# Attention before a gated feed-forward: the pairs' probabilities turned by VectorE and eight transfers instead of by TensorE

## The chip, the cores and the metric

The kernel runs on one core of a Trainium2 chip. The metric is the device time of one execution in microseconds, median of three runs; lower is better. TensorE does the matrix products, VectorE (DVE), ScalarE (ACT) and GpSimd (POOL) the rest; SyncE (SP) only issues DMAs.

## What is computed

```python
# q, k, v: (8, 8, 576, 64): batch, heads, tokens, head size; chunks of 64 tokens
scores = q_c @ k_c.T / sqrt(64)            # each chunk attends to itself
attn = exp(scores - max(scores)); attn = attn / (sum(attn) + 1e-9)
out = attn @ v_c
x = out.transpose(0, 2, 1, 3).reshape(4608, 512)
h = x @ w_in                               # 512 x 2048
g = h * clip(h + 3, 0, 6) / 6
return g @ w_out                           # 2048 x 512
```

## The kernel before

The 4608 tokens are nine blocks of 512. The large products run in three passes (L344 to L346) over operands that are split into a high and a low part. Blocks 0 to 2 go first, by ordinary products. The other six go in three pairs, (3, 4), (5, 6) and (7, 8): for a pair, seven products (numbered 1 to 7) on sums of quarters stand for eight, in the first product (with `w_in`) and again in the second (with `w_out`). The weights for that stream in through three `ws` buffers (`fetch`, L451), the operands are `xop` tiles made by `split` (L456 on ACT, L457 on DVE), and the gate is L637 on ACT and L638 on DVE. L605 are the sums of products in PSUM.

An `Attention` object is four heads of a block: 32 scores of 64 by 64. Its steps are `load_qk`, `load_v`, `scores` (32 matmuls, L228), `soft` (maximum L247, difference L249, exponential L251, sum L253, L257, L258, scaling L260, which leaves the probabilities in `e`), a turn of the probabilities, and `values` (32 matmuls, L310). While pair (3, 4) runs through its products, the four attentions of blocks 5 and 6 run between them; during pair (5, 6), those of blocks 7 and 8. These are the eight attentions of the title. For each of them `move` (L272) issues a DMA that copies `e` into the tile `words` (512 KB), so that its type may be fp32r; `turn` (L287) has TensorE transpose that in eight matmuls of 128 by 128 into PSUM (`two`), and `turned` (L293) has ACT copy them back over `e` as `aT`. The other ten attentions, of blocks 0 to 4, have no move and are transposed as float32 (L289). In what follows a pair's attentions are called the first to the fourth.

What runs when is written out by hand: the work of each engine is recorded slot by slot (`at` and `tick`); a slot is six matmuls of 128x512, and whatever is put at a slot is recorded for every engine, its DMAs on SP too, behind the matmuls of that slot. `STEADY` (one row for each of the four attentions) and `MOVES` hold the slots, counted from the pair's start; slots 0 to 55 are the first product, 56 to 111 the second. Each engine runs its own queue strictly in that order. `visit` records the `values` of one attention and behind them the `scores` of the next.

Each DMA counts on one of eight semaphores (`DMAHW0` to `DMAHW7`) in rotation. Before a DMA is issued on one, SP waits until the DMA that held it before, eight issues earlier, has landed.

Of the kernel before, what the change touches and what calls it, by code (L numbers as in the profile page):

```python
# [17 lines left out]
P = 128  # L18
CH = 64
# [50 lines left out]
TEMPS = {"p1": "w0_1", "u2": "w1_1", "u4": "w2_1"}  # L70
STEADY = ((-0.9, 8.1, 6.1, 0.2, 12.4, 13.9, 17.0, 19.1, 20.1), (13.1, 20.3, 20.1, 22.0, 23.5, 28.5, 32.2, 40.1, 41.1), (29.3, 53.1, 41.1, 42.4, 44.5, 46.4, 49.9, 54.1, 71.8), (65.6, 79.6, 71.8, 75.8, 77.2, 79.4, 79.5, 86.1, 87.6))
NEXT = (-37.5, -17.0, -24.4, -21.4, -18.0, -14.0, 0.5)
MOVES = (10.4, 33.1, 51.2, 79.8)
UNITS = (-2.9, -1.9, -1.8, -1.7, 4.0, 3.9, 5.4, 10.5, 12.5, 12.0, 13.2, 13.5, 16.6, 14.9, 15.4, 17.3, 25.9, 26.1, 27.5, 28.2, 28.5, 32.8, 35.3, 37.1, 39.2, 41.1, 39.3, 43.0)
# [6 lines left out]
def tile_kernel(ctx: ExitStack, tc: tile.TileContext, qk_in, v_in, weights, out):  # L81
# [105 lines left out]
    class Attention:  # L187


        def __init__(self, n, dp, psum=None):  # L190
# [5 lines left out]
            self.moved = None  # L196

# [19 lines left out]
        def scores(self, k=None):  # L217

            t = self.psum("a" if k == "a" else "s").rearrange("p a (c t) -> p a c t", t=CH)
            chunks = range(NB) if k is None else range(NB)[CHUNKS[k]]  # L220
            if k is None:
                self.s = t
            else:
                self.part[k] = t[:, :, :len(chunks)]
            for i, c in enumerate(chunks):
                for a, rows in enumerate(HALF):
                    for o in HALF:
                        PE.matmul(t[o, a, i, :], lhsT=self.qk[rows, c // 2, 0, c % 2, o],  # L228
                                  rhs=self.qk[rows, c // 2, 1, c % 2, o], start=not self.by_product or i == 0,
                                  stop=not self.by_product, skip_group_check=self.by_product)  # L230
# [31 lines left out]
        def subtract(self, k):  # L262

            for a in range(2):
                t = self.part[k][:, a]
                PE.matmul(t, lhsT=ident, rhs=self.m[:, a, CHUNKS[k]].unsqueeze(2).broadcast_to(list(t.shape)),
                          start=False, stop=True, skip_group_check=True)

        def move(self):

            self.moved = slot_tile("w3_1", [P, 2, NT], F32R, "words")
            nc.sync.dma_start(out=self.moved.bitcast(F32), in_=self.e.rearrange("p a c t -> p a (c t)"))  # L272

# [5 lines left out]
        def turn(self, heads):  # L279
            if heads[0] == 0:  # L280
                self.tp = self.psum("t").rearrange("p a (i t) -> p a i t", t=P)
                self.aT = self.e.rearrange("p a c t -> p (a c t)").rearrange("p (a i t) -> p a i t", a=2, t=P)
            for a in heads:
                for i in range(NB // 2):
                    o = slice(i * P, i * P + P)
                    if self.moved is not None:
                        PE.transpose(out=self.tp[:, a, i].bitcast(F32R), in_=self.moved[:, a, o], identity=unit_r[0])  # L287
                    else:
                        PE.transpose(out=self.tp[:, a, i], in_=self.e[:, a].rearrange("p c t -> p (c t)")[:, o], identity=ident)  # L289

# [9 lines left out]
        def multiply(self, heads):  # L300
# [5 lines left out]
            for a in heads:  # L306
                for i in range(NB // 2):
                    for s, rows in enumerate(HALF):
                        for o in HALF:
                            PE.matmul(self.po[s][o, a, i, :], lhsT=self.v[rows, a, i, o], rhs=self.aT[rows, a, i, o], start=True, stop=True)  # L310

# [71 lines left out]
    order.enter_context(tc.manual_schedule())  # L383
    unit_r = []

# [115 lines left out]

    lead = [Attention(n, 0) for n in range(NSTD + 2, NBLK, 2)]
    chain = [Attention(*which) for which in ((2, 0), (2, 1), (3, 0), (3, 1), (4, 0), (4, 1))] + lead[:1]
# [103 lines left out]
    def put_steady(first, base):  # L607

        pair = (first - NSTD) // 2 - 1
        four = [lead[pair]] + [Attention(first + k // 2, k % 2, steady_psum) for k in range(1, 2 * NDP)] + lead[pair + 1:pair + 2]  # L610
        rows = STEADY + (tuple(2 * SLOTS + t for t in NEXT),)
        for k, a in enumerate(four):
            soft = lambda i, a=a: lambda: a.soft(i)
            load_qk, load_v, scores, high, sub, total, mult, turn, values = (base + t for t in rows[k] + (0,) * (9 - len(rows[k])))
            if k:
# [7 lines left out]
                at(mult, soft(4))  # L623
            if len(rows[k]) < 9:
                return
            at(base + MOVES[k], a.move)
            at(turn, a.transpose)
            if k + 1 < len(four) and rows[k + 1][2] == rows[k][-1]:
# [25 lines left out]
    def first_products(box):  # L654
# [7 lines left out]
        for k, (n, ft) in enumerate(MIDDLE):  # L662
# [17 lines left out]
            if late:  # L680
                mm2(*late.pop(0))
                if not late:
                    std.close()
                    pools["L"] = ctx.enter_context(tc.tile_pool(name="late_l", bufs=1, reuse_waits="tile"))
                    unit_r.append(slot_tile("L", [P, P], F32R, "unit"))
                    ACT.copy(out=unit_r[0], in_=ident)
            tick(slot + 1)
# [239 lines left out]
```

## Time and profile before

| | |
|---|---|
| median of 3 runs | 785.77 us (784.89 to 786.03) |
| span of the profiled execution | 782.5 us |
| PE busy | 774.9 us, 99% of the span |
| DVE, ACT, POOL busy | 615.0 (79%), 375.6 (48%), 148.6 us (19%) |
| largest groups on PE | the three passes of the pairs' products, 608 matmuls of 128x512 in each line with `acc`, about 390 ns of latency each |

No time is given for the profiled execution as a whole other than its span, from the first instruction to the last; the median of the runs is 3.3 us above that. In a profile a matmul's duration is a latency, since matmuls are pipelined: what a matmul costs is the distance from its start to the next one's start.

### The profile page before, as it was taken

To read this page: it belongs to the slowest core of one execution; us is meant where nothing else is said; L and a number is where in the kernel's file an instruction comes from. 1 tells how busy PE (TensorE), PEld (TensorE's weight loads), DVE (VectorE), ACT (ScalarE), POOL (GpSimd) and SP (SyncE) were. 2 spreads that over 40 slices of the span, in tenths; PEclk is the share of its full clock that TensorE was granted. 3 is DMA by queue.
4 is the path that set the end of the run, shared out by engine and by line. 5 is a ranking of instruction groups with operands and counts; after the bars stand their busy time and mean duration, and the time that the engine had idled before them with its cause. 6 is when DMAs were issued, how large, how long until landed. Compare 5 with 4: busy or idle time off the path is not lost.

```text
span 782.5 us, 13689 instructions
## 1 busy us (share of the span) xinstructions
PE 774.9 (99%) x5601; PEld 636.9 (81%) x5601; DVE 615.0 (79%) x748; ACT 375.6 (48%) x494; POOL 148.6 (19%) x134
## 2 busy tenths in 40 slices
PE   8999999999999999999999999999999999999998
PEld 5888787888888888888888888888888888888886
DVE  7997868989699968686898886777997756669961
ACT  6997645535456434443654523444644323346330
POOL 0000013365471222322300002221100012221000
PEclk9999999999999999999999999999999999999999
DMA  9997977656867889976776778676756765665573
GB/s 367 408 408 258 345 258 262 238 177 218 334 251 276 295 291 330 347 270 213 268 268 226 258 230 272 220 262 209 263 195 216 247 217 188 194 202 209 183 240 115
DMA packets 50430, 200.12 MB, mean 256 GB/s; under 512 B 4544, under 2 KB 9152, under 8 KB 37312
## 3 DMA queue, kind: packets, MB, share of 16 engines
q1 hardware_dynamic: 50080, 198.99, 72.4%
q8 instruction: 44, 0.72, 0.4%
q10 hardware_dynamic: 288, 0.26, 0.1%
q14 instruction: 18, 0.15, 0.1%
HBM read 152.04 MB, written 42.99 MB: 249 GB/s over the span
## 4 chain that ended last, share of the span: by engine, by line
PE 95%; DVE 2%; DMA 2%; ACT 1%; issue 0%; SPq 0%; ACTq 0%
PE acc L344 23%; PE acc L346 22%; PE acc L345 22%; PE h L344 7%; PE h L346 7%; PE h L345 7%; PE h L310 2%; PE two L228 2%; PE two L289 1%; DMA x<-qk_in 1%; DMA a<-w 1%; PE two L287 1%; DVE w L182 0%; DVE e L260 0%; DVE u L168 0%; PE two L310 0%
## 5 line engine op out<-in xcount | busy, mean ns | idle before, releaser
L344 PE MATMUL acc<-xop,ws 128*128 128x512 f32 x608 | 237.9, 391 | 0.0
L346 PE MATMUL acc<-xop,ws 128*128 128x512 f32 x608 | 236.6, 389 | 0.0
L345 PE MATMUL acc<-xop,ws 128*128 128x512 f32 x608 | 236.6, 389 | 0.0
L344 PEld LDWEIGHTS acc<-xop,ws 128*128 128x128 f32 x608 | 114.1, 188 | 23.9 <-DVE g L638 0.3
L346 PEld LDWEIGHTS acc<-xop,ws 128*128 128x128 f32 x608 | 114.1, 188 | 23.6
L345 PEld LDWEIGHTS acc<-xop,ws 128*128 128x128 f32 x608 | 114.1, 188 | 23.4
L457 DVE TENSOR_TENSOR xop<-g,xop 128x1024 fp32r<-128x1024 f32 x96 | 117.1, 1252 | 18.9 <-ACT xop L456 18.9
L456 ACT CAST xop<-g 128x1024 fp32r<-128x1024 f32 x96 | 97.3, 1053 | 41.7 <-PE acc L346 25.8
L429 POOL TENSOR_TENSOR hl<-hl 128x256 f32<-128x256 f32 x64 | 56.8, 890 | 221.4 <-DVE hl L416 138.7
L723 POOL TENSOR_TENSOR g<-g 128x512 f32<-128x512 f32 x24 | 32.8, 1368 | 327.9 <-DVE g L638 327.9
L637 ACT ACTIVATE r<-acc,half 128x512 f32<-128x512 f32 x100 | 66.4, 687 | 57.8 <-DVE acc L605 42.2
L638 DVE SCALAR_TENSOR_TENSOR g<-r,acc 128x512 f32<-128x512 f32 x100 | 66.2, 680 | 29.7 <-ACT r L637 29.7
L344 PE MATMUL h<-xop,ws 128*128 128x512 f32 x176 | 68.7, 390 | 0.0
L346 PE MATMUL h<-xop,ws 128*128 128x512 f32 x176 | 68.5, 389 | 0.0
L345 PE MATMUL h<-xop,ws 128*128 128x512 f32 x176 | 68.5, 389 | 0.0
L637 ACT ACTIVATE r<-h,half 128x512 f32<-128x512 f32 x28 | 19.3, 690 | 99.6 <-DVE h L605 97.7
L605 DVE TENSOR_TENSOR u<-h,p 128x512 f32<-128x512 f32 x32 | 22.1, 690 | 36.6 <-PE h L346 27.1
L344 PE MATMUL acc<-x,w 128*128 128x512 f32 x112 | 44.7, 399 | 0.0
L346 PE MATMUL acc<-x,w 128*128 128x512 f32 x112 | 43.7, 390 | 0.0
L345 PE MATMUL acc<-x,w 128*128 128x512 f32 x112 | 43.7, 390 | 0.0
L251 ACT ACTIVATE e<-e 128x1024 f32<-128x1024 f32 (+1 forms) x18 | 18.3, 1014 | 43.8 <-DVE e L249 43.7
L346 PEld LDWEIGHTS h<-xop,ws 128*128 128x128 f32 x176 | 33.0, 188 | 6.9
(112 smaller groups left out, 1196.9 us busy)
## 6 DMA issues: line engine op xcount, KB each, us to landing
ws<-b SPq DMA_DIRECT2D x56, 1024.0 KB, 5.1
ws<-a SPq DMA_DIRECT2D x24, 1024.0 KB, 5.5
ws<-a SPq DMA_DIRECT2D x24, 768.0 KB, 5.0
qk<-qk_in SPq DMA_DIRECT2D x16, 1024.0 KB, 8.3
w<-w_in_out SPq DMA_DIRECT2D x12, 1024.0 KB, 17.3
v<-v_in SPq DMA_DIRECT2D x17, 512.0 KB, 6.2
out_t<-o SPq DMA_DIRECT2D x30, 256.0 KB, 6.2
b<-hl SPq DMA_DIRECT2D x12, 512.0 KB, 4.4
```

The costliest lines, as they stand in the source:

```text
L228: PE.matmul(t[o, a, i, :], lhsT=self.qk[rows, c // 2, 0, c % 2, o], rhs=self.qk[rows, c // 2, 1, c % 2, o], start=not self.by_product or i ...
L251: ACT.activation(out=flat(self.e), in_=src if self.by_product else flat(self.e), func=AF.Exp, scale=SCALE)
L344: PE.matmul(ps, lhsT=a_h, rhs=b_h, start=first, stop=False, skip_group_check=more)
L345: PE.matmul(ps, lhsT=a_h, rhs=b_l, start=False, stop=False, skip_group_check=more)
L346: PE.matmul(ps, lhsT=a_l, rhs=b_h, start=False, stop=last, skip_group_check=more)
L429: POOL.tensor_tensor(out=to, in0=x, in1=y, op=op)
L456: ACT.copy(out=t[:, :, 0], in_=src)
L457: DVE.tensor_tensor(out=t[:, :, 1], in0=src, in1=t[:, :, 0].bitcast(F32), op=ALU.subtract)
L605: return lambda: DVE.tensor_tensor(out=out, in0=x, in1=y, op=ALU.add)
L637: return (lambda: ACT.activation(out=r, in_=ps, func=AF.Relu, bias=half, scale=1.0 / 6.0), lambda: DVE.scalar_tensor_tensor(out=out, in0=r ...
L638: lambda: DVE.scalar_tensor_tensor(out=out, in0=r, scalar=1.0, in1=ps, op0=ALU.min, op1=ALU.mult))
L723: sub = lambda o, x, y: lambda: POOL.tensor_tensor(out=o, in0=x, in1=y, op=ALU.subtract)
```

## The change

For the eight attentions, the DMA into `words`, the eight transposes on TensorE and the copy on ACT go, and with them the fp32r unit matrix and the copy that made it. In their place `swap` has VectorE turn every 32 by 32 block of `e` in one instruction into a tile `t` (in the same slot of memory that `words` had), and `move` issues eight DMAs on SP, each of 32 partitions by 512 elements (64 KB), that put the turned blocks back over `e`, on the partitions where they belong. `scores` places the 64 by 64 blocks differently for that (as many matmuls, of the same sizes), and `values` reads each operand of 64 columns in two runs of 32. `SWAPS` and `MOVES` give the slots of the two steps; the loading of `q` and `k` of the fourth attention moves from slot 65.6 to 60.5.

```diff
-STEADY = (..., (65.6, 79.6, 71.8, 75.8, 77.2, 79.4, 79.5, 86.1, 87.6))
+STEADY = (..., (60.5, 79.6, 71.8, 75.8, 77.2, 79.4, 79.5, 87.6))
-MOVES = (10.4, 33.1, 51.2, 79.8)
+SWAPS = (7.5, 33.0, 61.9, 79.9)
+MOVES = (10.4, 35.1, 63.2, 80.8)
...
+            if self.blocks:
+                for g in range(NB):
+                    o, i = HALF[g // (NB // 2)], g % (NB // 2)
+                    for a, rows in enumerate(HALF):
+                        for c, to in enumerate(HALF):
+                            PE.matmul(t[to, a, g, :], lhsT=self.qk[rows, i, 0, c, o], rhs=self.qk[rows, i, 1, c, o], start=True, stop=True)
+                return
...
+        def swap(self, tag="w3_1"):
+            t = slot_tile(tag, [P, 2, 2 * NB, CH // 2], F32, "t")
+            DVE.transpose(out=t.rearrange("p j g t -> p g j t"), in_=self.e.rearrange("p a c (j t) -> p (a c) j t", j=2))
+            self.swapped = t.rearrange("p j g t -> p j (g t)")
+
         def move(self):
-            self.moved = slot_tile("w3_1", [P, 2, NT], F32R, "words")
-            nc.sync.dma_start(out=self.moved.bitcast(F32), in_=self.e.rearrange("p a c t -> p a (c t)"))
+            to = self.e.rearrange("p a c t -> p (a c t)").rearrange("p (i t) -> p i t", i=2)
+            for i in range(2):
+                for s in range(2):
+                    for j in range(2):
+                        rows = [slice(s * CH + k * CH // 2, s * CH + (k + 1) * CH // 2) for k in (i, j)]
+                        nc.sync.dma_start(out=to[rows[1], i], in_=self.swapped[rows[0], j])
+            self.aT = to.rearrange("p i (a o c t) -> p a c o i t", a=2, o=2, c=NB // 2)
...
-                            PE.matmul(..., rhs=self.aT[rows, a, i, o], start=True, stop=True)
+                            PE.matmul(..., rhs=self.aT[rows, a, i, HALF.index(o)] if self.blocks else self.aT[rows, a, i, o], start=True, stop=True)
...
+            at(base + SWAPS[k], a.swap)
             at(base + MOVES[k], a.move)
-            at(turn, a.transpose)
```

Line numbers of the changed kernel are some 13 to 15 higher behind the new lines: L344 to L346 are L360 to L362 there, L310 is L326, L457 is L472, L768 is L781, L451 is L466.

TensorE's queue where the first attention of blocks 5 and 6 is turned and used (`two<-unit,words` are the transposes, `h<-e,v` the values, `two<-qk` the scores of the next), before and now:

```order
L345 MATMUL acc<-xop,ws 128x512
L346 MATMUL acc<-xop,ws 128x512
L287 MATMUL two<-unit,words 128x128 x8
L344 MATMUL acc<-xop,ws 128x512
L345 MATMUL acc<-xop,ws 128x512
L346 MATMUL acc<-xop,ws 128x512
L344 MATMUL acc<-xop,ws 128x512
L345 MATMUL acc<-xop,ws 128x512
L346 MATMUL acc<-xop,ws 128x512
L310 MATMUL h<-e,v 64x64 x32
L228 MATMUL two<-qk 64x64 x32
```

```order
L361 MATMUL acc<-xop,ws 128x512
L362 MATMUL acc<-xop,ws 128x512
L360 MATMUL acc<-xop,ws 128x512
L361 MATMUL acc<-xop,ws 128x512
L362 MATMUL acc<-xop,ws 128x512
L326 MATMUL h<-e,v 64x64 x32
L231 MATMUL two<-qk 64x64 x32
```

The eight transposes are gone; nothing else on TensorE has another place.

VectorE's queue in the second product, around the new turn for the third attention (`g<-t` are differences between operands of the products, L768 then and L781 now), before and now:

```order
L768 TENSOR_TENSOR g<-t_3209,g 128x1024
L457 TENSOR_TENSOR xop<-g,xop 128x2x512
L768 TENSOR_TENSOR g<-t_3210,g 128x1024
L457 TENSOR_TENSOR xop<-g,xop 128x2x512
L768 TENSOR_TENSOR g<-t_3211,g 128x1024
```

```order
L781 TENSOR_TENSOR g<-t_3207,g 128x1024
L472 TENSOR_TENSOR xop<-g,xop 128x2x512
L781 TENSOR_TENSOR g<-t_3208,g 128x1024
L280 STREAM_TRANSPOSE t<-e 128x16x2x32
L472 TENSOR_TENSOR xop<-g,xop 128x2x512
L781 TENSOR_TENSOR g<-t_3209,g 128x1024
```

The turn (L280) stands behind the third of four such differences, and everything behind it is one instruction later.

SP's queue at the same place, with the semaphores that each DMA waits for (PE: a buffer that TensorE must have left), before and now:

```order
L451 DMA ws<-b 128x2048 [waits DMAHW6_49,PE_49]
L451 DMA ws<-b 128x2048 [waits DMAHW7_49,PE_49]
L451 DMA ws<-b 128x2048 [waits DMAHW1_49,PE_49]
L203 DMA qk<-qk_in 128x2048
L451 DMA ws<-b 128x2048 [waits DMAHW3_49,PE_49]
```

```order
L204 DMA qk<-qk_in 128x2048
L466 DMA ws<-b 128x2048 [waits DMAHW6_49,PE_49]
L290 DMA e<-t 32x512 [waits DVE_49]
L290 DMA e<-t 32x512 x2
L290 DMA e<-t 32x512 [waits DMAHW7_49]
L290 DMA e<-t 32x512 [waits DMAHW0_49]
L290 DMA e<-t 32x512 [waits DMAHW1_49]
L290 DMA e<-t 32x512 [waits DMAHW2_49]
L290 DMA e<-t 32x512 [waits DMAHW3_49]
L466 DMA ws<-b 128x2048 [waits DMAHW4_49,PE_49]
```

The eight transfers stand between two loads of weights here, the first waits for VectorE's turn, the others at most for the earlier holder of their semaphore, and `qk` has moved ahead of a load. (The one DMA of the third attention before, `words<-e`, stood in the first product.)

## Rows read from the trace of the kernel before

**Rows 1.** The page's first two parts; below, busy time in two stretches.

```profile
PE 774.9 (99%) x5601; PEld 636.9 (81%) x5601; DVE 615.0 (79%) x748; ACT 375.6 (48%) x494; POOL 148.6 (19%) x134
...
298.00:476.00 178.00, 178.00 (x1278) 147.71 (x1277) 142.21 (x171) 78.72 (x103) 29.94 (x26) 1.00 0.76 263
313.00:332.50 19.50, 19.50 (x211) 16.21 (x210) 12.96 (x20) 8.18 (x13) 7.08 (x8) 1.00 0.95 347
```

**Rows 2.** Timeline of PE, a first attention: start us, us, engine, line, operation, tiles.

```profile
325.66 0.39 PE L346 MATMUL acc<-xop,ws 128*128 128x512 f32 x1
325.89 0.80 PE L287 MATMUL two<-unit,words 128*128 128x128 f32 x8
326.52 0.46 PE L344 MATMUL acc<-xop,ws 128*128 128x512 f32 x1
326.82 0.40 PE L345 MATMUL acc<-xop,ws 128*128 128x512 f32 x1
...
328.05 1.16 PE L310 MATMUL h<-e,v 64*64 64x64 f32 x64
329.04 1.11 PE L228 MATMUL two<-qk 64*64 64x64 f32 x64
```

**Rows 3.** Instructions of L287: ns min/median/max, first and last start in us.

```profile
L287 PE MATMUL two<-unit,words x64: 221/249/253, 325.9 to 590.7; 128*128 128x128 f32 x64
```

**Rows 4.** Timeline of DVE where the third attention's turn will stand.

```profile
395.56 1.21 DVE L768 TENSOR_TENSOR g<-t,g 128x1024 f32<-128x1024 f32 x1
396.70 1.21 DVE L457 TENSOR_TENSOR xop<-g,xop 128x1024 fp32r<-128x1024 f32 x1
```

**Rows 5.** Timeline of PE: values of the third and the fourth attention.

```profile
403.36 1.16 PE L310 MATMUL h<-e,v 64*64 64x64 f32 x64
...
428.09 1.16 PE L310 MATMUL h<-e,v 64*64 64x64 f32 x64
```

**Rows 6.** Timeline of SP's queue: the kernel's first nine issues, later ones at the worst.

```profile
0.74 0.86 SPq L209 DMA_DIRECT2D qk<-qk_in  x2
...
3.69 1.52 SPq L149 DMA_DIRECT2D w<-w_in_out  x3
...
92.88 1.07 SPq L401 DMA_DIRECT2D b<-w  x1
```

**Rows 7.** DMA issues: count, size of one, median us from issue to landing.

```profile
out_t<-o SPq DMA_DIRECT2D x2, 128.0 KB, 1.7
...
ws<-b SPq DMA_DIRECT2D x56, 1024.0 KB, 5.1
```

**Rows 8.** Timeline of DVE: the fourth attention's scaling.

```profile
417.94 1.22 DVE L260 TENSOR_TENSOR e<-e,z 128x1024 f32<-128x1024 f32 x1
```

**Rows 9.** Timeline of SP's queue, a first attention, each with its landing in us.

```profile
313.84 0.32 SPq L451 DMA_DIRECT2D ws<-a  x1
...
DMA to landing us min/median/max: 7.2/7.2/7.2
318.29 0.55 SPq L203 DMA_DIRECT2D qk<-qk_in  x1
...
DMA to landing us min/median/max: 9.1/9.1/9.1
```

**Rows 10.** Timeline of SP's queue, a second attention; landing in us; PE's values there.

```profile
349.45 0.33 SPq L451 DMA_DIRECT2D ws<-a  x1
...
DMA to landing us min/median/max: 8.1/8.1/8.1
...
359.59 1.16 PE L310 MATMUL h<-e,v 64*64 64x64 f32 x64
```

**Rows 11.** Timelines of DVE and PE where the first attention's turn will stand.

```profile
311.64 0.69 DVE L638 SCALAR_TENSOR_TENSOR g<-r,acc 128x512 f32<-128x512 f32 x1 [0.17 <-ACT r L637]
...
313.28 0.69 DVE L605 TENSOR_TENSOR u<-acc,u 128x512 f32<-128x512 f32 x1
...
315.00 0.39 PE L344 MATMUL acc<-xop,ws 128*128 128x512 f32 x1
```

More of the change, by code (lines that the diff above doesn't have):

```diff
@@ L70 @@
 TEMPS = {"p1": "w0_1", "u2": "w1_1", "u4": "w2_1"}
-STEADY = ((-0.9, 8.1, 6.1, 0.2, 12.4, 13.9, 17.0, 19.1, 20.1), (13.1, 20.3, 20.1, 22.0, 23.5, 28.5, 32.2, 40.1, 41.1), (29.3, 53.1, 41.1, 42.4, 44.5, 46.4, 49.9, 54.1, 71.8), (65.6, 79.6, 71.8, 75.8, 77.2, 79.4, 79.5, 86.1, 87.6))
+STEADY = ((-0.9, 8.1, 6.1, 0.2, 12.4, 13.9, 17.0, 20.1), (13.1, 20.3, 20.1, 22.0, 23.5, 28.5, 32.2, 41.1), (29.3, 53.1, 41.1, 42.4, 44.5, 46.4, 49.9, 71.8), (60.5, 79.6, 71.8, 75.8, 77.2, 79.4, 79.5, 87.6))
 NEXT = (-37.5, -17.0, -24.4, -21.4, -18.0, -14.0, 0.5)
-MOVES = (10.4, 33.1, 51.2, 79.8)
+SWAPS = (7.5, 33.0, 61.9, 79.9)
+MOVES = (10.4, 35.1, 63.2, 80.8)
 UNITS = (-2.9, -1.9, -1.8, -1.7, 4.0, 3.9, 5.4, 10.5, 12.5, 12.0, 13.2, 13.5, 16.6, 14.9, 15.4, 17.3, 25.9, 26.1, 27.5, 28.2, 28.5, 32.8, 35.3, 37.1, 39.2, 41.1, 39.3, 43.0)
@@ L187, in tile_kernel, with __init__ @@
     class Attention:
-        def __init__(self, n, dp, psum=None):
+        def __init__(self, n, dp, psum=None, blocks=False):
+            self.blocks = blocks
             self.n, self.dp = n, dp
@@ L195, in __init__ @@
             self.by_product = False
-            self.moved = None
         def load_qk(self, qk=None):
@@ L285, in turn @@
                     o = slice(i * P, i * P + P)
[L286 to L289, printed above, removed]
+                    PE.transpose(out=self.tp[:, a, i], in_=self.e[:, a].rearrange("p c t -> p (c t)")[:, o], identity=ident)
         def turned(self, heads):
@@ L309, in multiply @@
                         for o in HALF:
-                            PE.matmul(self.po[s][o, a, i, :], lhsT=self.v[rows, a, i, o], rhs=self.aT[rows, a, i, o], start=True, stop=True)
+                            PE.matmul(self.po[s][o, a, i, :], lhsT=self.v[rows, a, i, o], rhs=self.aT[rows, a, i, HALF.index(o)] if self.blocks else self.aT[rows, a, i, o], start=True, stop=True)
         def multiplied(self, heads):
@@ L383, in tile_kernel @@
     order.enter_context(tc.manual_schedule())
-    unit_r = []
     words = dram.tile([P, NFP, 2, 512], F32, name="words")
@@ L500, in visit @@
         a.multiplied(range(2))
-    lead = [Attention(n, 0) for n in range(NSTD + 2, NBLK, 2)]
+    lead = [Attention(n, 0, blocks=True) for n in range(NSTD + 2, NBLK, 2)]
     chain = [Attention(*which) for which in ((2, 0), (2, 1), (3, 0), (3, 1), (4, 0), (4, 1))] + lead[:1]
@@ L609, in put_steady @@
         pair = (first - NSTD) // 2 - 1
-        four = [lead[pair]] + [Attention(first + k // 2, k % 2, steady_psum) for k in range(1, 2 * NDP)] + lead[pair + 1:pair + 2]
+        four = [lead[pair]] + [Attention(first + k // 2, k % 2, steady_psum, True) for k in range(1, 2 * NDP)] + lead[pair + 1:pair + 2]
         rows = STEADY + (tuple(2 * SLOTS + t for t in NEXT),)
@@ L613, in put_steady @@
             soft = lambda i, a=a: lambda: a.soft(i)
-            load_qk, load_v, scores, high, sub, total, mult, turn, values = (base + t for t in rows[k] + (0,) * (9 - len(rows[k])))
+            load_qk, load_v, scores, high, sub, total, mult, values = (base + t for t in rows[k] + (0,) * (8 - len(rows[k])))
             if k:
@@ L623, in put_steady @@
                 at(mult, soft(4))
-            if len(rows[k]) < 9:
+            if len(rows[k]) < 8:
                 return
+            at(base + SWAPS[k], a.swap)
             at(base + MOVES[k], a.move)
-            at(turn, a.transpose)
             if k + 1 < len(four) and rows[k + 1][2] == rows[k][-1]:
@@ L684, in first_products @@
                     pools["L"] = ctx.enter_context(tc.tile_pool(name="late_l", bufs=1, reuse_waits="tile"))
-                    unit_r.append(slot_tile("L", [P, P], F32R, "unit"))
-                    ACT.copy(out=unit_r[0], in_=ident)
             tick(slot + 1)
```

## The prediction

> **What bounds the kernel now.** I read the page's first part first: PE is busy 774.9 of the 782.5 us span, DVE 615.0 [rows 1]. In the stretch of the first four of the eight attentions, 298 to 476 us, PE is busy all 178.00 of 178.00 us at a granted clock of 1.00 (the upper of its two levels, 2.4 GHz), with DVE at 147.71 and the DMA engines at 0.76 [rows 1]. But busy PE is no proof that nothing waits, so I read the starts. Where nothing but 128x512 products runs, each starts 0.227 us after the one before (the row of L345 to the row of L346 would be 327.05 behind 326.82), and I found no larger step from 298 to 640 us except beside the attentions. So PE, and PE's queue alone, sets the end of this stretch: what leaves PE comes back in full, what DVE, ACT and SP gain is worth nothing, and what they lose costs only from where PE has to wait for it. The whole question is therefore whether the values (L310), the one place where PE meets the new path, find the turned probabilities in time.
>
> **Removed: 64 transposes.** L346 starts at 325.66, the eight transposes follow, and L345 starts at 326.82 with L344 ahead of it [rows 2]. That is 1.16 us for three steps, of which the two of products are 2 x 0.227. The eight transposes cost 1.16 - 0.45 = 0.71 us of PE. There are 64 instructions of L287 [rows 3], eight in each of the eight attentions: 8 x 0.71 = **5.65 us off the path**. The copy on ACT (L293) and the one 512 KB DMA into `words` go too; nobody waits for either, so I give nothing for them. `scores` and `values` keep their matmuls, as many of the same size. Values now read their moving operand as two runs of 32 elements. No row shows that form. A gain I exclude, since the count of columns is the same; half the rate would add what the 32 matmuls of the values take now, 329.04 - 328.05 = 0.99 us less the gap ahead of the scores, some 0.9 us each time [rows 2]. The transposes themselves and the products read longer runs and stream at a column a cycle, and 64 elements already are short runs; I take 0, and 0.9 as the bound.
>
> **Added on DVE: one turn.** No row of before shows a transpose on DVE. The nearest rows are others of 128x1024 in float32: 1.22 us for the scaling L260, 1.21 for L457, which start 1.14 apart [rows 4, 8]. Below it cannot well be, as it writes as many elements; the bound above is a turn at half the pace, 2.4 us. I take 1.2. At the first attention it stands ahead of the sums L605, about 311.5 us: DVE's queue there has small gaps, and the sum that starts at 313.28 would come about 0.6 us later; PE needs it at 315.00 [rows 11], which leaves about 1.0 us over its end of 313.97. Covered by 0.4 us, and not covered at 2.4 us, where some 0.8 us would show once. At the others DVE works 1.9 us or more ahead of PE. ACT and POOL see only a DVE that is 1.2 us later.
>
> **Added on SP: eight issues instead of one.** Each takes time on SP's queue, and PE waits for four of them ahead of the first values matmul and for the other four ahead of the third. The price of one: the only runs of issues in a row without waits are the first nine of the kernel, from 0.74 to 3.69 + 1.52 = 5.21 us [rows 6]: 4.47 / 9 = 0.50 us. A later one took 1.07 us at the worst [rows 6]. I take 0.50, keep 1.07 as the upper bound and, from the first two of the nine (0.86 us for both), 0.43 as the lower. From issue to landing: the smallest transfers are `out_t` of 128 KB, 1.7 us; a `ws` of 1 MB takes 5.1 [rows 7]. For 64 KB I take 1.7, since they are nearer to the first.
>
> **The third attention is where it gets late.** The turn stands ahead of the L457 at 396.70 [rows 4] and ends at 396.70 + 1.22 = 397.92. The first swap is issued then, the eighth 7 x 0.50 = 3.48 later at about 401.4 and landed at 403.1. The values stood at 403.36 [rows 5], and the first two attentions' transposes are no longer ahead of them, nor this one's: counted from the stream's own beginning of this attention, PE arrives 0.71 earlier, at 402.65 (what went before shifts DVE and SP alike). So PE waits 403.13 - 402.65 = 0.48 us. The same place comes in the second pair. **2 x 0.48 = 0.96 us given back.** The loads of `ws` behind the eight swaps are held about 3.8 us; two tiles' use (a tile serves 24 matmuls: 2 x 24 x 0.227 = 10.9 us) less a landing of 5.1 [rows 7] less 3.8 leaves 2.0 us. Covered.
>
> **The fourth.** The scaling of 417.94 [rows 8] is pushed by the third's turn (1.14), since DVE has no gap between; it and the new turn end at about 421.45. Eight issues and a landing: 421.45 + 3.48 + 1.7 = 426.65. PE's values stood at 428.09 [rows 5]; less two sets of transposes and plus the third's wait, that is 428.09 - 1.42 + 0.48 = 427.15. In time by 0.5 us.
>
> **The first and the second.** Here the eighth swap waits on the semaphore of a `ws` load issued just ahead. At the first attention that load went out at 313.84 and landed 7.2 us later, at 321.04 [rows 9]; before, SP issued the next `ws` and `qk` at about 318, so these come about 3 us later. That `qk` (318.29, 9.1 us to land, so 327.40) is wanted by the scores at 329.04 - 0.71 = 328.33 [rows 2, 9], 0.93 us to spare. Taken at its word that is 2.1 us of waiting, but the 9.1 us are a backlog: the engines are busy 0.95 of 313 to 332.5 us at 347 GB/s [rows 1], so a transfer put in later waits less in the backlog. I take 0; the bound is 2.8 us, once, since the second pair has over 1 us to spare. At the second attention the load of 349.45 lands at 357.55 and the values stood at 359.59 [rows 10]: the eighth swap lands by 357.55 + 1.7 = 359.25 against 359.59 - 0.71 = 358.88. At most 0.4 us; without `words` in the same backlog, 0. I take 0.
>
> **Sum.** -5.65 + 0.96 = -4.7 us: a span of 782.5 - 4.7 = 777.8. The median of the runs, 785.77, stands 3.3 us above the span of the profiled execution, and I carry that: **781.1 us**.
>
> Beside this, what the Trainium skill holds against such a change. The rows show transfers that overlap: the loads of 313.84 and the ones behind it are in flight together [rows 9]. The Trainium skill, "DMA: Bandwidth & Descriptors", § Rules for kernel authors, says that transfers under 64 KB mostly pay overhead and should be joined, and that two transfers to disjoint partition halves serialize, so that one of 128 partitions should be used. The swaps, of 64 KB and a quarter of the partitions each, stand at the edge of both; what one behind the other would make of the time is the fourth rival.
>
> **Rivals.** (1) *The gain is eaten up at DVE.* If a turn takes 2.4 us, the third comes out 0.48 + 1.2 late, the fourth about 0.7 less than another turn's 1.2 plus the first delay, some 1.3, the first of the first pair 0.8: 2 x 1.68 + 2 x 1.3 + 0.8 = 6.8 at the worst, and 5.5 where the waits at the third move PE away from the fourth; 785.77 - 5.65 + 5.5 = 785.6. For: no row shows the form. Against: every 128x1024 form in the rows takes 1.2 [rows 4, 8]. The first attention's `qk` (2.8) would end near there too, at 783.9. (2) *Slower: SP's issues are dear.* At 1.07 us each, the eight of the third attention end 7 x (1.07 - 0.50) = 4.0 us later, so PE waits 4.5 there and, the fourth being pushed no further, that is 2 x 4.2 more: 781.1 + 8.4 less what the fourth keeps free, 788.5. It decides from a wait of 2.83 per pair, or 0.48 + 7 x 0.34: from 0.83 us an issue on. For: a late issue took 1.07, and the landing is a guess by which 0.5 more counts double. Against: the issues of one queue without waits averaged 0.50 [rows 6]. (3) *Slower: values at half rate*: 8 x 0.9 = 7.2, 788.3. (4) *Slower: the eight land one behind the other*: 8 x 1.7 = 13.6 instead of 5.2 us from the turn, 8.4 more at the third and, less its 0.5 to spare, some 4 more at each other place: 2 x (8.4 + 3 x 3.5) less what overlaps, about +27, so near 808. Against: the load of 313.84 and the `qk` 4.45 us behind it were both in flight until 321.04 [rows 9].
>
> **How the numbers follow.** The forecast has 0.60, with its own range of 779.5 (issues at 0.43, which takes the third's wait to 0.48 - 7 x 0.07 = 0: 785.77 - 5.65 = 780.1, and half a microsecond of the runs' spread) to 783.5 (0.5 us more at the thirds, the second's 0.4, the `qk`). Rival 1 has 0.22: 783.5 to 787. Rival 2 has 0.12, rivals 3 and 4 0.03 each. About 0.2% (1.57 us, 784.2 to 787.3) is what a measurement of this kernel can tell from no change. Faster: 0.60 and 0.09 of rival 1, 0.69; same: 0.13 of rival 1; slower: 0.18 of the rest. The range takes in the forecast and rival 1, 779.5 to 787.0: 0.82.
>
> **What would show it right or wrong.** The L346 ahead of a first attention's old transposes should be followed by the next product 0.227 us later. The turn should be 1.2 us and not 2.4. The eight issues at the third attention should stand about 0.50 apart, the eighth landing 1.7 later, and the first values matmul there some 0.5 us late, with a releaser among the DMAs; values of the first, second and fourth should start on the stream's step. The values should still take about 0.9 us. Wrong it would be made by a wait of PE at the scores behind the first values (`qk`), by a `ws` that lands late behind the swaps, or by issues that wait on a semaphore that I have taken as free.

## The result, and the profile after

The changed kernel takes 790.39 us in the median (788.75 to 793.39, 8 runs) against 785.9 us before (784.62 to 788.82, 8 runs): a ratio of 1.0055, 95% interval 1.0034 to 1.0077. It is 4.5 us slower, where 4.7 us of gain were forecast, and lies outside the range.

The page's first part and the stretch with the first four of the eight attentions, to be read beside [rows 1] (start and end us, length, then busy us of PE, PEld, DVE, ACT, POOL, PE's granted clock, DMA share, GB/s):

```profile
PE 775.6 (98%) x5537; PEld 635.2 (80%) x5537; DVE 624.2 (79%) x756; ACT 367.7 (47%) x485; POOL 148.6 (19%) x134
...
298.00:476.00 178.00, 172.15 (x1219) 141.45 (x1218) 143.43 (x169) 73.98 (x96) 28.33 (x24) 0.99 0.75 255
```

PE was busy for all of that stretch before; now it stands still for 5.85 of 178 us, and a little of the rest runs at a lower clock. What it waits for, from the view of waits (engine, line, what ended the wait: us in total, times, longest):

```profile
PE h L326 <- DMA e<-t: 2.9, 4, 0.9
PE h L360 <- issue: 1.8, 1, 1.8
PE two L231 <- DMA qk<-qk_in: 1.6, 1, 1.6
PE h L326 <- DVE g L653: 0.7, 1, 0.7
PE h L326 <- issue: 0.3, 1, 0.3
```

The same view of the kernel before has no row there at all. I take each place apart in order. The size of a loss is the distance of starts from the last product ahead of the values to the first one behind the scores, less the 2.34 us that it was before. All losses are those of one profiled execution.

**The first attention.** SP's queue with the landing of `qk`, then PE's:

```profile
315.85 0.32 SPq L466 DMA_DIRECT2D ws<-a  x1
316.26 7.49 SPq L290 DMA_DIRECT2D e<-t  x8
...
324.42 0.46 SPq L204 DMA_DIRECT2D qk<-qk_in  x1
...
DMA to landing us min/median/max: 7.6/7.6/7.6
...
329.35 1.16 PE L326 MATMUL h<-e,v 64*64 64x64 f32 x64
332.15 1.16 PE L231 MATMUL two<-qk 64*64 64x64 f32 x64 [1.65 <-DMA qk<-qk_in]
```

The eight issues hold SP for 7.49 us, since the last of them waits until the load of 315.85 has landed. `qk`, which went out 4.45 us behind that load in [rows 9], now goes out 8.57 us behind it. It lands 7.6 us after its issue instead of 9.1 [rows 9], so 1.5 of the 4.1 us come back, and the scores wait for the rest. The values themselves start on time. Loss: 1.87 us.

**The second attention:**

```profile
352.61 0.32 SPq L466 DMA_DIRECT2D ws<-a  x1
352.98 9.17 SPq L290 DMA_DIRECT2D e<-t  x8
...
DMA to landing us min/median/max: 2.0/7.3/8.8
...
362.76 0.33 PE L326 MATMUL h<-e,v 64*64 64x64 f32 x4 [0.45 <-DMA e<-t]
363.80 1.09 PE L326 MATMUL h<-e,v 64*64 64x64 f32 x58 [0.71 <-DVE g L653]
```

The landing times are those of the eight `e<-t`. Each lands behind the loads that are already in the queues, 7.3 us after its issue in the median, and the eighth is not issued before the load of 352.61 is in, at 361.6. The second wait is put down to DVE's gate, but it is the eighth transfer that comes then (361.6 + 2.0 = 363.6). Loss: 1.55 us.

**The third attention.** DVE, SP with the landing of the eight, PE:

```profile
400.88 1.23 DVE L280 STREAM_TRANSPOSE t<-e 128x1024 f32<-128x1024 f32 x1
...
402.14 4.94 SPq L290 DMA_DIRECT2D e<-t  x8
407.19 1.03 SPq L466 DMA_DIRECT2D ws<-b  x2
...
DMA to landing us min/median/max: 1.9/2.0/2.0
...
407.37 0.33 PE L326 MATMUL h<-e,v 64*64 64x64 f32 x4 [0.34 <-issue]
408.59 1.09 PE L326 MATMUL h<-e,v 64*64 64x64 f32 x58 [0.89 <-DMA e<-t]
```

The turn takes 1.23 us, as a neighbour did in [rows 4]. SP waits for it, then issues the eight in 4.94 us; the engines are nearly empty, and each lands 2.0 us after its issue. The eighth is there at 408.5, PE came for it at 406.95. Loss: 1.63 us here and 1.94 us at the same place of the second pair. Behind the eight, two loads of weights go out at once.

**A stop that no semaphore explains.** Nine products behind the scores, in a row of products that wait for nothing (PE, then two stretches of 1 us in the columns above, then a row of the DMA queues from 412 to 414 us: packets, MB, share):

```profile
412.55 0.39 PE L362 MATMUL h<-xop,ws 128*128 128x512 f32 x1
414.75 0.50 PE L360 MATMUL h<-xop,ws 128*128 128x512 f32 x1 [1.81 <-issue]
...
416.64 0.63 PE L360 MATMUL h<-xop,ws 128*128 128x512 f32 x1
...
413.00:414.00 1.00, 0.00 (x0) 0.00 (x0) 1.00 (x2) 0.00 (x0) 0.00 (x0) 1.00 1.09 434
...
416.00:417.00 1.00, 1.00 (x3) 0.78 (x3) 1.00 (x2) 0.00 (x0) 0.00 (x0) 0.50 0.50 197
...
q8 instruction: 1, 0.02, 2.8%
```

The next product starts 2.20 us behind the last instead of 0.23. While PE stands, the DMA engines are full (1.09, 434 GB/s), and in that time one packet of 16 KB on a queue of instructions (q8) goes through. Soon after PE resumes, its granted clock falls to 0.50, the lower of its two levels (1.2 GHz), and eight products run at 0.427 us a step instead of 0.227. Loss: 1.97 us for the stop and 1.70 behind it, of which the eight products are 1.60.

The sum: 1.87 + 1.55 + 1.63 + 1.94 + 1.97 + 1.70 = 10.7 us lost, 5.65 won: 5.0 slower, beside 4.5 by the medians. All other visits (the fourth of each pair, the first and second of the second pair) run as before, in 2.34 us, or 1.41 at the very last, which has no scores behind it. The spans differ by more, 789.9 and 782.5: the profiled execution of the changed kernel was 2.0 us behind at the first of the eight attentions already, where the two kernels do the same, and 0.4 are left over.

### The profile page after: what moved, and what is told of

The parts are those of the page before. It is cut to its first block, busy times and chain, and to the rows that moved or that the text cites. A ratio compares the mean times of both kernels' runs of the same rounds, so it can differ in the third digit from the quotient of the medians.

```text
span 789.9 us, 13685 instructions
## 1 busy us (share of the span) xinstructions
PE 775.6 (98%) x5537; PEld 635.2 (80%) x5537; DVE 624.2 (79%) x756; ACT 367.7 (47%) x485; POOL 148.6 (19%) x134
## 4 chain that ended last, share of the span: by engine, by line
PE 87%; DVE 4%; DMA 4%; SPq 1%; issue 1%; ACT 1%; DVEq 0%; ACTq 0%
PE acc L360 21%; PE acc L362 20%; PE acc L361 20%; PE h L360 7%; PE h L362 7%; PE h L361 7%; DMA w<-w_in_out 3%; PE h L326 2%; SPq L290 1%; DVE xop L472 1%; PE two L231 1%; DMA qk<-qk_in 1%; PE two L305 1%; PE two L236 1%; DVE g L653 1%
## 5 line engine op out<-in xcount | busy, mean ns | idle before, releaser
L360 PE MATMUL acc<-xop,ws 128*128 128x512 f32 x608 | 237.6, 391 | 0.0
L362 PE MATMUL acc<-xop,ws 128*128 128x512 f32 x608 | 236.6, 389 | 0.0
L360 PEld LDWEIGHTS acc<-xop,ws 128*128 128x128 f32 x608 | 114.1, 188 | 24.9 <-DVE g L653 0.8
L362 PEld LDWEIGHTS acc<-xop,ws 128*128 128x128 f32 x608 | 114.2, 188 | 23.5
L472 DVE TENSOR_TENSOR xop<-g,xop 128x1024 fp32r<-128x1024 f32 x96 | 116.9, 1248 | 17.0 <-ACT xop L471 17.0
L360 PE MATMUL h<-xop,ws 128*128 128x512 f32 x176 | 69.4, 394 | 1.8 <-issue 1.8
L361 PE MATMUL h<-xop,ws 128*128 128x512 f32 x176 | 69.2, 393 | 0.0
L362 PE MATMUL h<-xop,ws 128*128 128x512 f32 x176 | 69.2, 393 | 0.0
L360 PE MATMUL acc<-x,w 128*128 128x512 f32 x112 | 44.7, 399 | 0.0
L362 PE MATMUL acc<-x,w 128*128 128x512 f32 x112 | 43.7, 390 | 0.0
L360 PEld LDWEIGHTS h<-xop,ws 128*128 128x128 f32 x176 | 33.5, 190 | 9.3 <-issue 2.2
```

The costliest lines, as they stand in the source:

```text
L360: PE.matmul(ps, lhsT=a_h, rhs=b_h, start=first, stop=False, skip_group_check=more)
L361: PE.matmul(ps, lhsT=a_h, rhs=b_l, start=False, stop=False, skip_group_check=more)
L362: PE.matmul(ps, lhsT=a_l, rhs=b_h, start=False, stop=last, skip_group_check=more)
L472: DVE.tensor_tensor(out=t[:, :, 1], in0=src, in1=t[:, :, 0].bitcast(F32), op=ALU.subtract)
```

## Experiments

The theory after these rows: all that was lost goes back to the eight issues on SP, to the wait for the load ahead of them, and to the loads behind them. The rivals were VectorE's turn, the new form of values and scores, and the DMA engines themselves.

**No transfers.**

```diff
...
-                        nc.sync.dma_start(out=to[rows[1], i], in_=self.swapped[rows[0], j])
-            self.aT = to.rearrange(...)
+            self.aT = self.swapped.rearrange(...)
```

> The eight transfers of each attention are left out; VectorE's turn stays, and the values read the turned tile itself, so part of the output is wrong (the blocks are not swapped). Theory (SP's queue): everything lost comes from the eight issues on SP, the waits for them and the loads that they hold, so without them the 5.65 us of the transposes come back in full: about 780.2 us, ratio 0.993, no wait of PE at the values. Rival 1 (VectorE): the turn delays the operands of the products; then the time stays above 784 us and PE waits for DVE. Rival 2 (the reading in two runs of 32, or the new order of the scores, is slower): the values or the scores take more than 2.34 us together and the time stays above 784 us.

Measured: 779.39 us, ratio 0.9933 (0.9916 to 0.9950). The view of PE's waits is empty again. The first stretch:

```profile
298.00:476.00 178.00, 178.00 (x1258) 146.97 (x1257) 149.44 (x179) 74.68 (x99) 30.91 (x26) 1.00 0.74 252
```

DVE does more in it than before (149.44 against 142.21 us) and PE waits for nothing. The visits take the old 2.34 us. The turn is free, and the form of values and scores is too. Both rivals fall, and the first term of the prediction stands: the transposes are worth their 5.65 us, within the interval.

**Transfers that nobody waits for.** All eight are issued, the values read the turned tile:

```diff
-            self.aT = to.rearrange(...)
+            self.aT = self.swapped.rearrange(...)
```

> All eight transfers are issued as in the changed kernel, but the values read VectorE's turned tile and not what the transfers bring, so PE waits for none of them (part of the output is wrong for that). Theory (SP's queue): two kinds of loss, the values' own waits (about 1.5 us at the second attention, 1.6 and 1.9 at the two third ones, 5.1 in all) and loads that the burst holds on SP (1.9 us at the scores behind the first attention, and the stop of 2 us behind the third with 1.6 us at half clock). Only the first kind goes: 790.4 - 5.1 = about 785.3 us (784 to 786.5). Rival (the wait is all): 780.2 us, as without transfers.

Measured: 781.31 us, ratio 0.9959 (0.9943 to 0.9974), 4 us better than expected and within 1.1 us of the rival's 780.2. PE's waits are these:

```profile
PE two L231 <- DMA qk<-qk_in: 1.1, 1, 1.1
PE h L360 <- DVE o L800: 0.3, 1, 0.3
```

The late `qk` remains, 1.34 us by the starts: the burst alone costs that. The other losses go with the values' waits, as the rival said. The stop behind the third attention, which I had counted with the held loads, is not there, though the loads go out in a bunch here too. So it needs more than the burst.

**The instruction stream cut elsewhere.** The warming products at the kernel's start, in four pieces each:

```diff
-            PE.matmul(idle, lhsT=a[:, :P], rhs=b, ...)
+            for k in range(4):
+                PE.matmul(idle[:, k * P:k * P + P], lhsT=a[:, :P], rhs=(columns k * P to k * P + P of b), ...)
```

> The changed kernel with each of the warming products of 512 columns at the kernel's start cut into four of 128 columns: the same columns on PE, but about a hundred more instructions ahead of everything else, so that the stream of instructions is cut at other places where it is loaded. Theory (the stop of 2 us behind the third attention, in a row of products that wait for no semaphore, is a load of instructions that came late while the DMA engines were full): the stop goes or moves to another place, and with it the 1.6 us at half clock; 787 us. Rival (the stop belongs to the loads of weights held by the burst): it stays behind the third attention, 790.4 us.

Measured: 788.51 us, ratio 1.0036 (1.0020 to 1.0051). In the profiled execution the stop of the first pair is gone. In the second pair one has come at the like place, where the changed kernel has none, and this time the clock stays at 1.00:

```profile
573.07 0.39 PE L362 MATMUL h<-xop,ws 128*128 128x512 f32 x1
574.74 0.50 PE L363 MATMUL h<-xop,ws 128*128 128x512 f32 x1 [1.28 <-issue]
```

The order of all work is the same; ahead of it stand 75 more products and 75 more loads of PE's weights. So the stop hangs on where the stream of instructions is cut, as a late load of instructions would. That profile is one of the faster: in seven of the 12 executions the granted clock was 0.997 or 0.998, as in seven of the changed kernel's eight, so most still had a stretch at the lower clock, and by its time (1.0020 to 1.0051 beside 1.0034 to 1.0077) this kernel cannot be told from the changed one.

The packets on queue q8 say more. In the changed kernel, over the 31.6 us ahead of the stop, the part on queues has no row for it, though the DMA engines moved nothing for a while; in about the same stretch of the run with unread transfers, which has no stop, it has one (the changed kernel from 380.7 to 412.3 us: GB/s in 40 slices, then the one queue; the other run from 376.4 to 409.5):

```profile
GB/s 0 145 114 342 446 373 430 213 166 321 373 249 135 93 114 384 425 436 425 404 425 156 384 425 322 0 0 0 78 88 83 125 119 88 83 197 342 415 467 363
...
q1 hardware_dynamic: 1436, 7.70, 70.3%
...
q8 instruction: 1, 0.02, 0.2%
```

Counted over all thirteen traces, the starts of two packets on q8 lie at most 231 of PE's products apart (each product with its weight load), except at four places, with 254 or 255. These four are the stops: the one above, this one, and the same place in the run with halves and in the repeat. The packet itself is not slow (0.90 us at the stop, 0.88 to 1.42 elsewhere in that kernel and the one before). But it begins only 0.1 to 0.7 us ahead of the last product before the stop. The Trainium skill, "Runtime: NRT & Kernel Launch", § Instruction fetch mechanics, says that instructions are refilled in blocks of 16 KiB, 256 of them, and that crossing a boundary is mostly hidden. The traces agree on the block (44 packets in the changed kernel, 0.72 MB, for 5537 products and as many weight loads, 252 instructions to a packet), and on "mostly": all but these four crossings are hidden, and these cost 1.4 to 2.0 us.

**The changed kernel again,** for a second trace:

> The changed kernel once more, unaltered, for a second trace. Theory: the late loads and late transfers are in it again, within 0.5 us of each (1.9 at the scores behind the first attention, 1.5 at the second's values, 1.6 and 1.9 at the thirds); the stop of 2 us behind the third attention, if it is a load of instructions that comes late, may be there or not.

It took 789.25 us in its one run. PE waits 2.8 us for `e<-t` and 1.7 for `qk`, as before to 0.1 us, and the stop is at the same place and as long (1.8 us), with the lower clock behind it.

Other traces are less alike. In the next run, which alters nothing ahead of 380 us, the first attention loses 0.18 us instead of 1.87; in the run with the shifted stream the first loses 1.06 and the second nothing instead of 1.55. The load just ahead of the burst lands at another distance each time. So the price of these two places in one trace is a sample.

**The third attention earlier, turn and transfers.**

```diff
-SWAPS = (7.5, 33.0, 61.9, 79.9)
-MOVES = (10.4, 35.1, 63.2, 80.8)
+SWAPS = (7.5, 33.0, 56.9, 79.9)
+MOVES = (10.4, 35.1, 58.2, 80.8)
```

> Only the third attention's turn and transfers are put five slots earlier (slots 56.9 and 58.2 instead of 61.9 and 63.2), behind another load of weights. Theory: the values of both third attentions find their blocks (1.6 and 1.9 us back), and the two ws loads and the qk behind the burst are no longer issued together, so the stop of PE behind it goes too (up to 3.6 us of the profiled execution): 784 to 787 us. Rival (the transfers are late whenever they are issued, because they share the DMA engines with the loads): the thirds stay late and the time stays at 790.

Measured: 787.50 us, ratio 1.0032 (1.0015 to 1.0048), half a microsecond above what was expected. The values of the thirds no longer wait. But now the burst stands ahead of a load of weights on SP while VectorE has not yet come to the turn:

```profile
382.75 0.32 SPq L466 DMA_DIRECT2D ws<-b  x1
390.49 4.94 SPq L290 DMA_DIRECT2D e<-t  x8
395.53 0.53 SPq L466 DMA_DIRECT2D ws<-b  x1
...
400.91 0.47 PE L360 MATMUL acc<-xop,ws 128*128 128x512 f32 x1 [1.72 <-DMA ws<-b]
```

The loads are 12.8 us apart instead of 5.4 (a tile serves 24 products), and PE waits 1.7 us for one. The second pair loses as much (1.99 us), and the clock falls there.

**The third turn earlier alone.** Only `SWAPS`' third entry, 61.9 to 56.9; the transfers keep their slot.

> Only the third attention's turn on VectorE is five slots earlier (56.9 instead of 61.9); its transfers keep their place on SP behind the same load of weights (63.2). Theory: SP no longer waits for VectorE there, the eight go out right behind that load, 4 to 5 us earlier than in the changed kernel, the values of both third attentions find them (3.6 us back in all), and the next two loads go out one by one, so PE does not stop behind them: 790.4 - 3.6 - up to 3.6 = 783 to 787 us. Rival (the eight issues hold SP for 5 us wherever they stand, and a load behind them is late, as with turn and transfers both earlier): a stop of about 2 us in each pair remains, 787.5 us.

Measured: 783.62 us, ratio 0.9982 (0.9969 to 0.9995): now faster than before.

```profile
395.17 0.32 SPq L466 DMA_DIRECT2D ws<-b  x1
395.54 5.37 SPq L290 DMA_DIRECT2D e<-t  x8
401.00 5.37 SPq L466 DMA_DIRECT2D ws<-b  x2
```

The eight go out right behind a load, SP is free again 5.8 us behind it, and the two loads behind the burst start some 5 us apart. No third visit waits, and there is no stop behind it. What is left is the first attention (1.98 us), the second (1.61), and now also the fourth ones (0.58 and 1.19), where PE arrives earlier and the transfers do not.

**Halves around a load,** at the first and the second attention: `move` takes half of its loop at a time, at slots 10.4 and 13.9, 33.9 and 35.1.

> Only the first and the second attention's transfers are split in two halves of four, with a load of weights (and at the first one qk too) issued between the halves, so that no transfer waits for the semaphore of the load issued just ahead and qk is issued earlier. Theory (semaphore of the load ahead, and loads held behind it): the wait at the scores behind the first attention (1.9 us) and at the second attention's values (1.5 us) go, the thirds stay: about 787 us. Rival (the DMA engines are the bound there and order on SP changes nothing): 790 us and the same waits.

Measured: 789.42 us, ratio 1.0057 (1.0041 to 1.0073); expected were 787. At the first attention `qk` came in time, but then the second half of the transfers was behind `qk` in the same backlog, and the values waited 1.68 us instead. The second lost 0.88 instead of 1.55, and 0.7 for a load of weights ahead of it. The thirds' waits, the stop and the half clock are in this trace too, about as long as in the changed kernel. Here the rival is right for the most part: in these two places, with the engines full, another order on SP changed who was late.

**`qk` ahead of the burst,** with the early third turn: `load_qk` from slot 13.1 to 10.3.

> Eight transfers, the third turn early (as in the run with that alone, 783.6 us), and the load of the second attention's qk put ahead of the first attention's transfers (slot 10.3 instead of 13.1). Theory (qk comes late only because it stands behind the burst on SP): the wait of 1.9 us at the scores behind the first attention goes, 781.7 us; the eighth transfer now waits for qk's landing, and a load of weights behind it may lose part of that again (up to 1.5 us). Rival (qk is late because the DMA engines are full there, wherever it is issued): 783.6 us and the same wait.

Measured: 784.09 us, ratio 0.9978 (0.9964 to 0.9991), no different from 783.62. The scores no longer wait for `qk`. The 0.49 us left there are a load of weights that the burst held, since its last transfer now waits for `qk`. The second still loses 1.61, and the fourth ones 0.54 and 1.35. Ahead of the first attention PE lost 0.7 us (0.5 in some other traces), because VectorE's sums waited there for an earlier store to land:

```profile
301.40 0.69 DVE L800 TENSOR_TENSOR o<-h,u 128x512 f32<-128x512 f32 x1 [2.63 <-DMA out_t<-o]
...
330.83 0.50 PE L360 MATMUL acc<-xop,ws 128*128 128x512 f32 x1 [0.41 <-DMA ws<-a]
```

The term moved as expected, the time did not. As the first attention lost only 0.18 us in another trace with `qk` in its old place, one trace does not settle that the place made the difference.

**GpSimd's queue,** with the early third turn: `nc.gpsimd.dma_start` for the 64 transfers, at slots 8.4, 33.9, 58.2, 80.8.

> The third turn is five slots earlier and all 64 transfers are issued by GpSimd's queue instead of SP's, right behind the turns (slots 8.4, 33.9, 58.2, 80.8). Theory (SP's queue is the cause): SP issues its loads as without transfers, nothing is held, and the transfers have 5 us and more ahead of the values everywhere: about 781 us, near the 779.4 without transfers. Rival (the transfers themselves load the DMA engines or land late, whoever issues them): PE waits at the second attention's values as before, above 783 us. A second rival: issues on GpSimd are so slow that GpSimd's own sums come late and PE waits for them.

Measured: 787.27 us, ratio 1.0020 (1.0006 to 1.0033), so the theory's 781 was wrong. An issue takes 0.50 us there and SP is free. But at the fourth attention a load of weights goes out on SP at the same moment, and the transfers land behind it (the landing of the eight, then PE):

```profile
DMA to landing us min/median/max: 4.4/5.1/5.8
...
429.49 0.33 PE L326 MATMUL h<-e,v 64*64 64x64 f32 x4 [2.06 <-DVE xop L472]
430.01 1.09 PE L326 MATMUL h<-e,v 64*64 64x64 f32 x58 [0.19 <-DMA e<-t]
```

They take 5.1 us instead of the 2.0 that SP's took on empty engines; the fourth visits lose 2.63 and 2.49 us, the first 0.62, the second 0.75, and a load of weights comes 1.1 us late ahead of it. (The first row names VectorE, but in the second pair the same wait, 2.1 us, is put down to `e<-t`.) So SP's queue is not the whole cause: here transfers that SP does not issue are late beside a load. Whether that is the DMA engines alone is not shown, since no burst of GpSimd's met empty engines.

**Four transfers instead of eight.** Half of the blocks stay on their partitions. ACT copies the turned tile over `e`, and only the others are sent; the third turn is early:

```diff
-SWAPS = (7.5, 33.0, 61.9, 79.9)
+SWAPS = (7.5, 33.0, 56.9, 79.9)
...
+            ACT.copy(out=to, in_=self.swapped)
             for i in range(2):
                 for s in range(2):
-                    for j in range(2):
-                        (one transfer of block j, i)
+                    (one transfer, for j = 1 - i)
```

> Four transfers instead of eight: the blocks that stay on their partitions are copied by ACT (a copy of 128x1024 from the turned tile, as ACT made before the change), SP issues only the four that change partitions; the third turn is five slots earlier. Theory (number of issues and the semaphore of the load ahead): SP is held 2.5 us instead of 5, no transfer has to wait for the load issued just ahead, so qk and ws go out about as before the change: 780 to 783 us. Rival (one load late is enough, or ACT's copy holds ACT's queue): PE still waits at the scores of the first attention or for ACT, 785 us or more.

Measured: 780.10 us (778.84 to 780.72), ratio 0.9933 (0.9920 to 0.9945). It is faster than both kernels and as fast as the one without transfers. SP at the first and at the third attention, and ACT's copy ahead of the latter:

```profile
313.61 0.32 SPq L466 DMA_DIRECT2D ws<-a  x1
314.02 2.75 SPq L290 DMA_DIRECT2D e<-t  x4
...
318.07 0.43 SPq L204 DMA_DIRECT2D qk<-qk_in  x1
...
388.45 1.05 ACT L286 COPY e<-t 128x1024 f32<-128x1024 f32 x1
...
390.31 0.32 SPq L466 DMA_DIRECT2D ws<-b  x1
390.69 2.42 SPq L290 DMA_DIRECT2D e<-t  x4
```

Four issues take 2.4 to 2.8 us here (3.4 at most), none waits for the load just ahead, and `qk` goes out 4.46 us behind that load, as before the change (4.45). All eight visits take what they took before the change.

**Four transfers, the third turn where the change put it.**

> As the kernel with four transfers and ACT's copy, but the third turn stays where the change put it (slot 61.9). Theory (the number of issues and the semaphore of the load ahead cost at the first and the second attention, the place of the turn at the third): the first and second attentions are in time, and the third ones late by a little: turn until 402.1 in the changed kernel's time, copy 1.1, three more issues at 0.63, a landing of 2.0 make 407.1 against the 406.95 at which PE got there, so 0.2 to 1 us each: 780.5 to 782 us. Rival (the place of the third turn is what counts most): the thirds lose 1.5 us and more each, and the time is over 783 us.

Measured: 785.77 us, ratio 1.0000 (0.9988 to 1.0013), a miss by 4 us. The thirds' values are nearly in time, but ACT's copy waits for the late turn, and ACT's casts of the operands stand behind it (ACT, then PE):

```profile
397.50 1.05 ACT L286 COPY e<-t 128x1024 f32<-128x1024 f32 x1 [7.73 <-DVE t L280]
...
400.51 0.51 PE L360 MATMUL acc<-xop,ws 128*128 128x512 f32 x1 [0.86 <-ACT xop L471]
401.77 0.50 PE L361 MATMUL acc<-xop,ws 128*128 128x512 f32 x1 [0.76 <-DVE xop L472]
```

With the restarts that is 2.2 us ahead of the values in each pair, and the fourth ones lose 0.65 and 0.59. The rival's time came, by a wait that neither side had named. Both halves of the faster kernel are needed: fewer transfers for the first and second attention, an earlier turn for the third.

## Why the prediction was wrong, step by step

The term that failed is what PE waits. The prediction gave back 0.96 us, all of it at the thirds, and took the first and the second attention at 0 and the loads behind the burst as covered. The traced execution gave back 10.7: 1.87 and 1.55 at the first and the second, 3.57 at the thirds, 3.67 in the stop. Its own first sign of being wrong, a wait at the scores for `qk`, came true.

- **What bounds.** Right. The 147.71 us that it gives for DVE are the weight loads' (PEld); DVE has 142.21 [rows 1]. Nothing rests on that.
- **Removed.** Right: 5.65 us by the sum, and 0.9933 without the transfers.
- **The turn on DVE.** Right: 1.23 us against 1.2, and covered. Rival 1 (a turn of 2.4 us) and rival 3 (the values at half rate) fall with it.
- **The third attention.** The mechanism was right, both terms a little small. Seven steps of issue took 4.36 us (0.62 each) where 0.50 was taken from loads of the kernel's start [rows 6], and a landing took 2.0 where 1.7 was taken from [rows 7]. So 1.63 and 1.94 us instead of 0.48 each. Rival 2 had named this mechanism, but with 0.83 us an issue as its point; by itself it did not decide.
- **The first attention.** This step failed by its choice. It saw that the eighth swap waits for the load ahead and that `qk` comes 3 us later, worked out 2.1 us of waiting "at its word", and then took 0 because the backlog would let `qk` catch up. It went out 4.1 us later, not 3, and caught up by 1.5 (7.6 us to land instead of 9.1): 1.87 us.
- **The second attention.** At most 0.4 us, taken as 0; measured 1.55. The eighth swap did wait for the load of weights and then for its own 2.0. The load itself landed 9.0 us after its issue instead of 8.1 [rows 10]; with 0.3 more for the last landing these 0.9 make up the difference. That the burst of the first attention had pushed the backlog back is likely, but not shown. Each attention was costed against a trace in which the one before it had not been changed.
- **"Covered" behind the third.** The loads of weights themselves did come in time. But the stop of PE came there, with the half clock behind it: 3.7 us in no term of the sum. No row of before shows such a stop, so this part could not have been read from them.
- **The fourth.** In time, by luck. PE came to it late, by the third's wait in both pairs and by the stop in the first. With that gone (the third turn earlier alone) the fourths lose 0.58 and 1.19 us. The prediction's own sum, with the measured 0.62 us an issue and 2.0 to land, gives 421.45 + 4.34 + 2.0 = 427.8 against 427.15, which is 0.6 late; that covers the first of the two, not the second. The second pair's first two: right, in time.
- **Rival 4.** At the third attention the eight overlap, 0.62 us apart with 2.0 us to land each, and do not serialize. The Trainium skill, "DMA: Bandwidth & Descriptors", § Rules for kernel authors, says that transfers to disjoint partition halves do. The trace agrees only behind loads: at the second attention the first six land one behind the other, 0.17 us apart, from 361.8 us on, and 0.17 is far from the rival's 1.7.

The slower side had 0.18. Three waits were each taken at the kind end of their own bounds. With the other ends (2.8, 0.4, and half a microsecond at each of the thirds) the sum is 781.1 + 2.8 + 0.4 + 1.0 = 785.3; the stop's 3.7 lie beyond any of them. The 2.8 for `qk` has no working, and the forecast's upper end of 783.5 is too low for the terms that it names, since with `qk` at 2.1 they come to 784.6. Rival 2's 2 x 4.2 should be 2 x 4.0.

## What is left open

That the stop is a load of instructions that comes late rests on its place, which moved with the cut of the stream, and on the distance of the packets, which is 254 or 255 products at the stops and nowhere else. Why that packet begins so late is open. Full engines do not explain it: in the 31.6 us in which none began they moved nothing for 2.4 us, and the transfers that nobody waited for filled them as well and had no stop. Why PE resumes only 1.4 to 1.5 us behind the packet's end, and why the losses at the first and the second attention vary as they do between traces, is open too.

## What to carry to other kernels

A step that moves work from the bound engine to DMAs should be counted first in issues on the queue that also feeds the bound engine: what stands behind the burst, and which earlier load its last transfer waits for. If a wait is worked out from rows and then argued away by a backlog, its price belongs in the sum. A step that is in time only because another was late is not in time. And when transfers are late, first ask which need not be sent: half of these moved no data between partitions, and the engine that had copied before could copy them.

## What the hardware showed that I had not expected

- A transfer of 64 KB between partitions takes 0.62 us of SP's queue in a row, where a load of 1 MB takes 0.32, and lands 1.9 to 2.0 us after its issue on empty engines and 7.3 us (median) behind loads.
- GpSimd's queue issues the same transfer every 0.50 us, faster than SP.
- PE can lose 1.4 to 2.0 us without any semaphore, at the places where a block of 16 KB of instructions begins 254 or 255 products behind the last one; up to 231 apart it lost nothing of the kind. Which places these are depends on how many instructions lie ahead.
- After the stop PE's granted clock fell to its lower level for 3.4 us in three traces, not at once but 0.2 to 1.0 us after PE had resumed; after the one in the second pair with the stream cut elsewhere it did not.
